# Gating the first two chunks as one group, first fills on VectorE, and weight loads cut into column pieces

## The chip, the cores and the metric

The kernel runs on one core of one Trainium2 chip. The metric is the device time of one execution in microseconds (us), lower is better. Five engines work side by side, each on its own instruction stream in order: TensorE (PE, with its weight loads shown as PEld), VectorE (DVE), ScalarE (ACT), GpSimd (POOL) and SyncE (SP). SP and POOL also issue the DMAs.

## What is computed

The reference has two blocks. The first is a gated linear attention over 4 sequences of 768 steps, 8 heads of 48 channels: a complex gate per step and channel, limited in magnitude, decays a 48x48 state, and each output is the query times the state. The second is a mixer on the 384-wide result.

```python
mag = sqrt(a_re*a_re + a_im*a_im)
scale = minimum(mag, 0.999) / (mag + 1e-06)
a = (a_re + 1j*a_im) * scale
for t in range(768):                       # per batch, head
    S = a[t][:, None] * S + outer(k[t], v[t])
    y[t] = q[t] @ S.real
x = y as (batch, 768, 384)
u = x + ((x.T @ U) @ V).T                  # U: 768x32, V: 32x768
out = u + maximum(u @ w_ch1, 0) @ w_ch2    # 384x1536, 1536x384
```

The four mixer weights arrive as 64-bit doubles and are turned into 32-bit floats on the chip.

## The kernel before

**Chunks.** Each sequence is cut into six chunks of 128 steps, 24 in all. A chunk passes through these steps. *Gates* (`gates`): magnitudes through squares, Ln and Exp on ScalarE with adds on VectorE, sums over blocks on TensorE (`es ps`, `tot`), then angles (Arctan on ScalarE, a running sum on TensorE into `ph`, wrapped into `F`), then sine and cosine into `cs`. *Prep* (`prep`): queries and keys weighed by `es`, multiplied by `cs` into `QKC`, transposed by TensorE (`tr`) and copied to `QK` by ScalarE. *Levels and rest* (`chain`): many small products (`inner`, `corners`, `ks ps`, `dk`, `y`), with VectorE rescaling `QK` in place between them, end in `xo`.

**Gates come in groups.** `GROUPS` says which chunks are gated together: `(0, 1)`, `(1, 2)`, then pairs. For a pair each ScalarE and VectorE step is one 768-wide instruction, for a single chunk a 384-wide one. Each group loads two ScalarE function tables (`switch`), one for magnitudes and one for angles.

**The mixer** (`mixer`) takes two chunks at a time once a whole sequence has its `xo`: `mixed`, `uTp`, then the long products `up` and `down`. Later mixers use schemes with fewer products (`few`). Weights (`single`) are loaded by SP as raw doubles into one of two `raw` buffers in `stage`, 768 KB each for the six pieces of `w1` and the six of `w2`. Six VectorE instructions rebuild the float's high part and a correction, and a DMA from POOL adds the correction to `w` in place.

**The order of everything** is made by a planner that runs when the kernel is built (`Plan`). Every operation is entered with an engine, an assumed duration, an urgency class and what it reads and writes; the table `URGENCY` gives a number for each class and index, and each engine takes the most urgent ready operation. The result is one fixed stream per engine. Where the planner expects TensorE to have nothing to do before the first `mixing` operation has been planned, it puts a filler in the stream, a 128x128 product of the identity with itself named `spare` (`idle`, line 1232). Fillers are real instructions: TensorE executes all of them in order, whether it would have been idle or not.

**The start.** POOL sets up `ident`, fills the constant parts of `QKC`, the three `T`, two `AT` and two `DG` tiles (lines 392 to 407), and only then makes `mid` and `total` from the loaded `prefix` (lines 415 to 434).

Of the kernel before, what the change touches and what calls it, by code (L numbers as in the profile page):

```python
# [12 lines left out]
U32 = mybir.dt.uint32  # L13
# [9 lines left out]
GC = 2  # L23
# [3 lines left out]
    "w1": {0: 577.09, 1: -1319.32, 2: 484.43, 3: -236.69, 4: 471.82, 5: -1058.73, 6: 187.51},  # L27
    "w2": {0: -111.09, 2: 522.21, 4: 896.97, 6: -52.37, 8: 604.14, 10: 640.8, 12: -317.28},
    "gates": {0: -265.04, 1: 268.17, 2: 43.76, 4: -996.63, 6: 89.37, 8: 509.61, 10: -55.71, 12: 809.99, 14: -95.12,
        16: 160.61, 18: -122.91, 20: -425.54, 22: -1729.17},  # L30
    "angles": {0: -126.72, 1: -84.17, 2: -1567.87, 4: -1150.68, 6: -325.13, 8: 105.31, 10: 61.73, 12: 732.88,
        14: -1148.2, 16: 655.25, 18: 538.84, 20: -116.45, 22: 233.15},
    "prep": {0: -1639.87, 1: -367.99, 2: -1022.47, 3: -12.47, 4: -106.92, 5: -436, 6: -74.87, 7: 260.1, 8: -1682.29,
        9: 278.7, 10: 47.08, 11: 569.46, 12: -1452.21, 13: -249.3, 14: -287.97, 15: -363.52, 16: -269.7,
        17: -1664.43, 18: -240.93, 19: 153, 20: -1089.48, 21: -198.95, 22: -127.5, 23: 757.32},
    "levels": {0: 731.75, 1: -318.03, 2: 17.02, 3: -430.68, 4: -436.08, 5: -170.38, 6: 221.56, 7: 124.72, 8: -1567.59,
        9: -1453.16, 10: -1698.36, 11: -60.78, 12: 502.58, 13: 523.21, 14: -1475.59, 15: 515.81, 16: -1265.88,
        17: 487.77, 18: -263.92, 19: 16.81, 20: 723.89, 21: -1759.83, 22: -1111.46, 23: -160.12},
    "rest": {0: 468.93, 1: -1086.12, 2: 24.25, 3: -218.54, 4: -1119.41, 5: -346.92, 6: 0.68, 7: -1700.8, 8: 681.55,
        9: -376.72, 10: -229.72, 11: -305.85, 12: -1069.62, 13: 601.71, 14: -282.72, 15: 204.95, 16: 59.77,  # L40
        17: 552.08, 18: -62.45, 19: 466.03, 20: -1105.96, 21: -351.77, 22: -1688.33, 23: 463.92},
# [147 lines left out]
def kernel(  # L189
# [47 lines left out]
    GROUPS = [(0, 1), (1, 2)] + [(n, n + GC) for n in range(2, NT, GC)]  # L237
    NG = len(GROUPS)

    PAIRED = 6  # L240
# [5 lines left out]
    AT_ONCE = (0, 1, 2, 3)  # L246
    WP = 768

# [64 lines left out]
    def SP(cost, *a, **kw):  # L313
        plan.add("SP", max(cost, 0.65), *a, late=2.0 if cost > 0.65 else 1.4, **kw)
# [77 lines left out]
    nc.gpsimd.memset(QKC, 0.0)  # L392
# [5 lines left out]
    for n in range(3):  # L398
        TS.append(singles.tile([DQ, GC, H * NTOT], FP, name="T%d" % n))
        nc.gpsimd.memset(TS[n], 1.0)  # L400
    for n in range(3):
        VP.append(singles.tile([128, H, D], FP, name="VP%d" % n))
    for n in range(2):
        AT.append(singles.tile([128, H, HC], FP, name="AT%d" % n))
        DG.append(singles.tile([128, H, BLK], FP, name="DG%d" % n))
        nc.gpsimd.memset(AT[n], 0.0)
        nc.gpsimd.memset(DG[n], 0.0)
# [37 lines left out]
    def load_a(g):  # L445
        lo, hi = GROUPS[g]
        for nm, src in (("ar", a_re), ("ai", a_im)):
            for i in range(lo, hi):
                SP(c_dma(DM), ("load", (0, 0.5, 3)[g] if g < 3 else lo + 3), lambda nm=nm, src=src, i=i: nc.sync.dma_start(
                    out=get(nm, g)[:, i - lo], in_=rows(src, i)), writes=[(nm, g, i)])  # L450
# [12 lines left out]
    def single(p, rank, to, o, pieces):  # L463
# [12 lines left out]
        for a, at, end in zip(pieces, ends, ends[1:]):  # L476
            SP(c_dma(2 * (end - at)), rank_l, lambda a=a, at=at, end=end: nc.sync.dma_start(
                out=get("raw", p)[:, at:end].rearrange("p (c m) two -> p c (m two)", c=a.shape[1]), in_=a.bitcast(U32)),
               writes=[("raw", p, at)])
# [51 lines left out]
    def gates(g):  # L531


        lo, hi = GROUPS[g]
        W = (hi - lo) * DM
        R1, R2 = ("gates", lo), ("angles", lo)
        ca, cd = c_act(W), c_dve(W)
        x, y, l, n, z, ar, ai = names = [(nm, g) for nm in ("x", "y", "l", "n", "z", "ar", "ai")]

        def t(b):  # L540
            a = get(*b)
            return (a.rearrange("p c h d -> p (c h d)") if b[0][0] == "a" else a)[:, 0:W]

        def of(b, i):
            return get(*b)[:, (i - lo) * DM:(i - lo + 1) * DM]

        def magnitudes():
            ring(l, "GL", GL)
            ACT(ca, R1, lambda: act(t(x), t(ar), AF.Square), [ar], [x])
            ACT(ca, R1, lambda: act(t(y), t(ai), AF.Square), [ai], [y])  # L550
            DVE(cd, R1, lambda: add(t(x), t(x), t(y)), [y], [x])
            DVE(c_one(W), R1, lambda: nc.vector.tensor_scalar(out=t(x), in0=t(x), scalar1=M2LO, scalar2=M2HI, op0=OP.max,
                                                              op1=OP.min), [], [x])
            ACT(ca, R1, lambda: act(t(n), t(ar), AF.Abs), [ar], [n])
            table(ca, R1, lambda: act(t(l), t(x), AF.Ln), [x], [l])
            table(ca, R1, lambda: act(t(x), t(l), AF.Exp, scale=0.5), [l], [x])
            DVE(cd, R1, lambda: add(t(x), t(x), t(n)), [n], [x])
            table(ca, R1, lambda: act(t(y), t(l), AF.Exp, scale=-0.5, bias=leps), [l], [y])
            table(ca, R1, lambda: act(t(y), t(y), AF.Ln, bias=1.0), [], [y])

            ACT(ca, R1, lambda: act(t(l), t(l), AF.Relu, scale=-0.5, bias=lmax), [], [l])
            DVE(cd, R1, lambda: nc.vector.scalar_tensor_tensor(out=t(l), in0=t(l), scalar=LNMAX, in1=t(y), op0=OP.subtract,
                                                               op1=OP.add), [y], [l])
            table(ca, R1, lambda: act(t(x), t(x), AF.Ln), [], [x])
            table(ca, R1, lambda: act(t(x), t(x), AF.Exp, scale=-1.0), [], [x])
            DVE(cd, R1, lambda: mul(t(x), t(x), t(ai)), [ai], [x])
            ACT(ca, R1, lambda: act(t(n), t(ar), AF.Sign, bias=tiny), [ar], [n])
            for i in range(lo, hi):
                within(i)

        def within(i):
            ps, es = ("es ps", i), ("es", i)
            psum(ps, "T", [128, DM], [128, 512])
            buffer(es, "es", 3, [128, 2, DM])
            PE(0.65, R1, lambda: nc.tensor.matmul(out=get(*ps), lhsT=mid, rhs=of(l, i), start=True, stop=True),  # L575
               [l, ("mid", 0)], [ps, ("sums", g, i)], takes=[es], steps=2)
            for u in range(2):
                table(c_act(DM), R1, lambda u=u: act(get(*es)[:, u], get(*ps), AF.Exp, scale=1.0 - 2 * u), [ps], [es + (u,)])

        def totals():  # L580
# [3 lines left out]
            for i in range(lo, hi):  # L584
                of_blocks(i)
# [6 lines left out]
        def of_blocks(i):  # L592
# [15 lines left out]
        def turns():  # L608

            table(ca, R2, lambda: act(t(x), t(x), AF.Arctan), [], [x])  # L610
            DVE(cd, R2, lambda: nc.vector.scalar_tensor_tensor(out=t(z), in0=t(x), scalar=math.pi / 4, in1=t(n),  # L611
                                                               op0=OP.subtract, op1=OP.mult), [x, n], [z])
            ACT(ca, R2, lambda: act(t(z), t(z), AF.Identity, scale=1.0 / math.pi, bias=fourth), [], [z])
            for i in range(lo, hi):
                angles(i)

        def angles(i):
# [6 lines left out]
            first = i < NCH  # L624
            if where(i)[1] > 0 and not first:
                POOL(1.0, R2, lambda: nc.gpsimd.dma_start(out=of(z, i)[0:1], in_=fo(i - 1)[CH - 1:CH], accum_op=OP.add),
                     [("F", i - 1)], [zi], late=2.6)
# [3 lines left out]
            carry = first and i > 0  # L631
# [9 lines left out]
        def waves():  # L641
            cs = ("cs", g)
            buffer(cs, "cs", 2, [128, GC, H, 2, D])

            def half(u):
                return get(*cs).rearrange("p c h u d -> p (c h) u d")[:, 0:W // D, u]
            fs = [("F", i) for i in range(lo, hi)]
            ft = heads(F.rearrange("p c m -> p (c m)")[:, lo % GC * DM:lo % GC * DM + W])
            ACT(ca, R2, lambda: act(half(0), ft, AF.Abs), fs, [cs + (0,)])
            table(ca, R2, lambda: act(half(1), ft, AF.Sin, scale=2.0 * math.pi), fs, [cs + (1,)])  # L650
            table(ca, R2, lambda: act(half(0), half(0), AF.Sin, scale=-2.0 * math.pi, bias=quarter), [], [cs + (0,)])
# [9 lines left out]
    def prep(i):  # L661
        R1 = "prep", i
        g = group_of(i)
        qk, QK = ("qk", i), ("QK", i)
        buffer(QK, "QK", 3, [DQ, 2, H, CH])
# [4 lines left out]
        for u in range(2):  # L670
# [4 lines left out]
                [qk, ("cs", g)], [qkc])  # L675
# [521 lines left out]
    for g in range(NG):  # L1197
# [8 lines left out]
        if g:  # L1206
            totals()
        else:
            later = [totals]
# [78 lines left out]
```

## Time and profile before

| | before |
|---|---|
| median of 3 runs | 705.47 us (704.29 to 705.83) |
| profiled execution, its own time | 704.41 us |
| span of the profile (first to last instruction) | 702.6 us |
| PE busy | 681.1 us, 97% |
| of it fillers (`spare`) | 61.4 us, 219 products |
| DVE / ACT / POOL busy | 540.1 / 418.1 / 51.8 us |
| mean granted TensorE clock | 0.990 of full |

In the profile every 32-bit matmul shows as two records, so 438 `spare` records are 219 products. Busy time counts overlapped records once. "Issue" is time in which an engine waited for nothing that the profile shows.

### The profile page before, as it was taken

The page shows a single profiled execution, that of the slowest core. Times are in us where ns is not written, and L with a number is a line of the kernel's source. Part 1 is how long each engine was busy: PE and PEld are TensorE (multiplying, and loading weights), DVE is VectorE, ACT ScalarE, POOL GpSimd, SP SyncE. Part 2 cuts the span into 40 slices and gives each one's busy share as a digit, 9 for nine tenths or more (in the row PEclk, how much of TensorE's full clock was granted, in tenths as well). Part 3 has the DMA queues.
Part 4 walks back from the last instruction along what each step waited for, and adds up shares of the span by engine and source line. Part 5 has one row for each costly group of instructions (what it writes and reads, how often), then busy time and mean ns, then how long its engine had stood idle before and what let it go on. Part 6 is the DMA issues. An engine that isn't in the chain of part 4 may idle for free.

```text
span 702.6 us, 27047 instructions
## 1 busy us (share of the span) xinstructions
PE 681.1 (97%) x12148; PEld 601.0 (86%) x12148; DVE 540.1 (77%) x877; ACT 418.1 (60%) x778; POOL 51.8 (7%) x92
## 2 busy tenths in 40 slices
PE   7989998999999999999999999999999999999998
PEld 6877877877688888879888888889999999899997
DVE  5899998888898887759678487879887787455734
ACT  6786987678797687977784953651624415041230
POOL 5110000011000010001000000000000000000000
PEclk9999999799999999999999999999999999999999
DMA  7876855498424343252334032040121000000000
GB/s 185 172 184 149 186 103 141 91 209 176 99 51 90 68 94 76 41 109 53 63 77 93 9 67 59 10 98 26 23 42 35 14 27 17 18 7 24 7 18 22
DMA packets 165267, 53.24 MB, mean 76 GB/s; under 512 B 154080, under 2 KB 160416, under 8 KB 165152
## 3 DMA queue, kind: packets, MB, share of 16 engines
q1 hardware_dynamic: 161072, 42.26, 27.7%
q0 software_dynamic: 4080, 9.27, 5.6%
q8 instruction: 95, 1.56, 0.9%
q14 instruction: 20, 0.16, 0.1%
HBM read 33.59 MB, written 4.72 MB: 55 GB/s over the span
## 4 chain that ended last, share of the span: by engine, by line
PE 79%; ACT 9%; DVE 7%; issue 3%; DMA 1%; SPq 0%; DVEq 0%; ACTq 0%
PE down L1105 21%; PE few L974 12%; PE up L916 12%; PE inner L716 6%; PE tr L682 5%; ACT gate L326 3%; PE dk L802 3%; PE y L841 3%; PE spare L1232 2%; PE ks ps L787 2%; PE down L1062 2%; PE es ps L575 2%; PE ph L632 2%; PE tot L601 2%; PE y L833 2%
## 5 line engine op out<-in xcount | busy, mean ns | idle before, releaser
L329 DVE TENSOR_TENSOR QK<-QK,T 112x1024 f32<-112x1024 f32 x120 | 145.8, 1221 | 6.5 <-PE corners L766 5.3
L916 PE MATMUL up<-uT,w 128*128 128x256 f32 x432 | 98.7, 381 | 0.0
L916 PEld LDWEIGHTS up<-uT,w 128*128 128x128 f32 x432 | 80.7, 190 | 12.0 <-DVE uT L906 0.2
L326 ACT ACTIVATE gate<-gate 128x768 f32<-128x768 f32 (+1 forms) x91 | 71.0, 792 | 6.2 <-DVE gate L611 2.0
L1105 PE MATMUL down<-w,h 128*128 128x192 f32 x396 | 73.2, 330 | 0.0
L982 ACT COPY h<-few 128x512 f32<-128x512 f32 x36 | 20.8, 584 | 85.2 <-PE few L974 85.1
L685 ACT COPY QK<-tr 112x512 f32<-112x512 f32 x96 | 52.0, 588 | 32.6 <-PE tr L682 32.3
L1105 PEld LDWEIGHTS down<-w,h 128*128 128x128 f32 x396 | 63.9, 190 | 2.7 <-issue 1.3
L1232 PE MATMUL spare<-ident 128*128 128x128 f32 x438 | 61.4, 289 | 2.1 <-POOL ident masks.py:199 1.5
L332 DVE TENSOR_TENSOR h<-few,h 128x512 f32<-128x512 f32 x54 | 37.2, 691 | 30.2 <-PE few L974 26.2
L1232 PEld LDWEIGHTS spare<-ident 128*128 128x128 f32 x438 | 55.1, 198 | 5.9 <-issue 1.9
L716 PEld LDWEIGHTS inner<-QK 112*32 112x32 f32 x4608 | 45.9, 110 | 16.4 <-issue 10.7
L716 PE MATMUL inner<-QK 112*32 112x16 f32 (+1 forms) x4608 | 51.2, 190 | 4.9 <-issue 4.5
L682 PE MATMUL tr<-ident,QKC 128*112 128x128 f32 x384 | 51.9, 275 | 1.2 <-ACT QK L685 0.8
L329 DVE TENSOR_TENSOR QKC<-qk,cs 128x768 f32<-128x768 f32 x48 | 45.9, 956 | 9.3 <-PE tr L682 6.6
L332 DVE TENSOR_TENSOR xo<-down,xo 128x192 f32<-128x192 f32 (+1 forms) x79 | 29.8, 388 | 27.0 <-PE down L1105 25.2
L682 PEld LDWEIGHTS tr<-ident,QKC 128*112 128x112 f32 x384 | 42.3, 133 | 6.1 <-ACT QK L685 1.8
L974 PE MATMUL few<-gate,w 128*128 128x128 f32 x336 | 43.1, 277 | 0.0
L1049 POOL DMA_DIRECT2D out_dram<-xo x32 | 17.9, 560 | 338.9 <-DVE xo L332 278.8
L850 ACT COPY xo<-y 64x192 f32<-64x192 f32 x96 | 30.1, 313 | 19.2 <-PE y L841 16.0
L722 DVE COPY_PREDICATED DG<-mask,inner 128x128 f32<-128x128 int32 (+1 forms) x72 | 24.6, 344 | 20.4 <-PE inner L716 20.3
L974 PEld LDWEIGHTS few<-gate,w 128*128 128x128 f32 x336 | 40.0, 192 | 0.3
(131 smaller groups left out, 1272.0 us busy)
## 6 DMA issues: line engine op xcount, KB each, us to landing
stage<-in_moe_w_ch_dram SPq DMA_DIRECT2D x12, 768.0 KB, 6.5
gate<-in_a_re_dram SPq DMA_DIRECT2D x24, 192.0 KB, 3.2
gate<-in_a_im_dram SPq DMA_DIRECT2D x24, 192.0 KB, 4.3
qk<-in_q_dram SPq DMA_DIRECT2D x24, 192.0 KB, 4.0
qk<-in_k_dram SPq DMA_DIRECT2D x24, 192.0 KB, 4.4
VP<-in_v_dram SPq DMA_DIRECT2D x24, 192.0 KB, 3.3
w<-stage POOLq DMA_DIRECT2D x12, 384.0 KB, 5.7
T<-E SPq DMA_DIRECT2D x44, 96.0 KB, 2.5
```

The lines of the kernel that those rows point to most:

```text
L326: return nc.scalar.activation(out=o, in_=i, func=f, **kw)
L329: nc.vector.tensor_tensor(out=o, in0=a, in1=b, op=OP.mult)
L332: nc.vector.tensor_tensor(out=o, in0=a, in1=b, op=OP.add)
L682: nc.tensor.transpose(out=get(*ps)[0:DQ, j], in_=get(*qkc)[:, hh * HH + j].rearrange("p u d -> p (u d)")[:, 0:DQ], identity=ident)
L685: ACT(c_act(HH * CH) - 0.05, R1, lambda u=u, hh=hh, ps=ps: nc.scalar.copy(out=get(*QK)[:, u, hh * HH:(hh + 1) * HH], in_=get(*ps)[0:DQ]), ...
L716: nc.tensor.matmul(out=get(*ps)[js, h], lhsT=k_of(h)[:, js], rhs=part(q_of(h)[:, js], "p"), start=True, stop=True, tile_position=(0, j * BLK))
L722: nc.vector.copy_predicated(out=to, mask=part(mask[:, n], "p").unsqueeze(1).to_broadcast(list(to.shape)), data=a if hf < 8 else a.rearrang ...
L850: ACT(c_act(HH * D), RR, lambda r=r, u=u: nc.scalar.copy(out=get(*xi).rearrange("p (a u d) -> p a u d", u=2, d=D)[r * HC:(r + 1) * HC, :, ...
L916: nc.tensor.matmul(out=get(*ps)[:, e], lhsT=w1[:, f, (ff + e) * 128:(ff + e + 1) * 128], rhs=get(*uT)[:, f], start=(f == 0), stop=(f == KD ...
L974: nc.tensor.matmul(out=get(*ps)[:, q], lhsT=w()[:, q * 128:(q + 1) * 128], rhs=v[0](), start=(n == 0 and q == 0), stop=True, skip_group_ch ...
L1105: nc.tensor.matmul(out=get(*to)[:, part], lhsT=x(j), rhs=y[:, j], start=(first and j == 0), stop=(j == KH - 1), skip_group_check=not first)
L1232: nc.tensor.matmul(out=spare[0], lhsT=ident, rhs=ident, start=True, stop=True)
```

## The change

- `GROUPS` becomes twelve pairs; the first two chunks are now one group with one pair of table loads. Inside that group, `PARTS` keeps the two chunks as separate 384-wide instructions with their own urgencies; all other groups have one part of 768.
- Totals of the first group are no longer put off until after the next group's table load.
- `PAIRED` and `AT_ONCE` move by one, since group numbers moved by one; they mean the same chunks as before.
- The eight first fills go from POOL to VectorE.
- A weight load becomes four DMAs of 192 doubles per row (192 KB each) in place of one of 768 KB.
- The gate loads of both first chunks lead SP's stream.
- `URGENCY` has new numbers throughout, so every engine's stream is ordered anew.

```diff
-    "w1": {0: 577.09, 1: -1319.32, 2: 484.43, 3: -236.69, 4: 471.82, 5: -1058.73, 6: 187.51},
+    "w1": {0: 646.97, 1: 441.39, 2: -1086.15, 3: 866.49, 4: 669.69, 5: 511.71, 6: 120.17},
...
-    GROUPS = [(0, 1), (1, 2)] + [(n, n + GC) for n in range(2, NT, GC)]
+    GROUPS = [(n, n + GC) for n in range(0, NT, GC)]
+    PARTS = [[(n, n + 1) for n in range(GC)]] + [[g] for g in GROUPS[1:]]
-    PAIRED = 6
+    PAIRED = 5
-    AT_ONCE = (0, 1, 2, 3)
+    AT_ONCE = (0, 1, 2)
+    SPLIT = 192
...
-    nc.gpsimd.memset(QKC, 0.0)
+    nc.vector.memset(QKC, 0.0)
...
-        nc.gpsimd.memset(TS[n], 1.0)
+        nc.vector.memset(TS[n], 1.0)
...
-        nc.gpsimd.memset(AT[n], 0.0)
-        nc.gpsimd.memset(DG[n], 0.0)
+        nc.vector.memset(AT[n], 0.0)
+        nc.vector.memset(DG[n], 0.0)
...
-                SP(c_dma(DM), ("load", (0, 0.5, 3)[g] if g < 3 else lo + 3), ...
+                SP(c_dma(DM), ("load", i / 20 if g == 0 else 3 if g == 1 else lo + 3), ...
...
+            m = a.shape[2]
+            if m <= SPLIT:
...
+            for c in range(a.shape[1]):
+                for lo in range(0, m, SPLIT):
+                    hi = min(lo + SPLIT, m)
+                    o_at = at + c * m + lo
+                    SP(c_dma(2 * (hi - lo)), rank_l, lambda ...: nc.sync.dma_start(
+                        out=get("raw", p)[:, o_at:o_at + hi - lo], in_=a[:, c, lo:hi]...),
+                       writes=[("raw", p, o_at)])
...
-        if g:
-            totals()
-        else:
-            later = [totals]
+        totals()
```

Built, the two kernels differ in these instruction counts: 196 fillers for 219; 24 table loads for 26; 8 fills on VectorE and none of these on POOL; 48 weight loads for 12 (beside the two of U and V); 48 stores of totals for 52. Every other kind of instruction has the same count and size, and the streams differ in order.

## The prediction

> **What bounds the kernel now.** I read the page's busy times and slices first, then the windows by stage, then PE's waits and the timeline at the places where PE stood still.
>
> ```profile
> PE 681.1 (97%) x12148; PEld 601.0 (86%) x12148; DVE 540.1 (77%) x877; ACT 418.1 (60%) x778; POOL 51.8 (7%) x92
> ...
> PE   7989998999999999999999999999999999999998
> DVE  5899998888898887759678487879887787455734
> ...
> PEclk9999999799999999999999999999999999999999
> ...
> L1232 PE MATMUL spare<-ident 128*128 128x128 f32 x438 | 61.4, 289 | 2.1 <-POOL ident masks.py:199 1.5
> ```
>
> PE looks full from the start, but 61.4 of its 681.1 us are fillers, and all fillers stand before the first `up`. Full rows of DVE lie in the same stretch, and the clock row has one slice below full.
>
> ```profile
> 0.00:20.00 20.00, 14.99 (x107) 13.37 (x108) 11.05 (x25) 12.41 (x23) 10.65 (x33) 0.91 0.82 190
> 20.00:112.00 92.00, 85.33 (x1896) 72.44 (x1894) 87.61 (x129) 74.91 (x137) 6.29 (x7) 1.00 0.70 155
> ...
> 116.00:119.00 3.00, 0.00 (x1) 0.00 (x0) 1.43 (x2) 2.83 (x4) 0.00 (x0) 1.00 0.49 136
> ...
> 120.40:130.70 10.30, 9.98 (x204) 8.31 (x193) 8.66 (x11) 3.80 (x12) 0.00 (x0) 0.50 0.31 72
> 130.70:152.00 21.30, 21.04 (x456) 17.11 (x455) 18.66 (x30) 15.19 (x31) 2.89 (x3) 1.00 0.66 136
> 152.00:650.00 498.00, 495.56 (x8940) 437.23 (x8939) 381.53 (x619) 293.25 (x551) 30.31 (x46) 1.00 0.27 58
> ```
>
> The columns after the length are PE, PEld, DVE, ACT and POOL busy, granted clock, DMA share, GB/s. From 152 us on PE has 2.4 us of idle in 498: that part is bound by PE's real work, which the change leaves alone. From 20 to 112 DVE is busy 95% of the time. So the time is decided by how early the first mixer can start, and in that front part DVE (then ACT) sets the pace while PE pads with fillers.
>
> ```profile
> PE inner L716 <- issue: 4.5, 3, 3.1
> ...
> PE es ps L575 <- DVE mask L440: 3.6, 1, 3.6
> ...
> 5.83 1.73 DVE L552 TENSOR_SCALAR gate<-gate 128x384 f32<-128x384 f32 x1
> ...
> 11.13 1.53 PE L575 MATMUL es ps<-GL,mid 128*128 128x384 f32 x2 [3.56 <-DVE mask L440]
> ...
> 119.11 0.45 PE L716 MATMUL inner<-QK 112*32 112x32 f32 x30 [3.10 <-issue]
> ...
> 152.24 7.93 PE L916 MATMUL up<-uT,w 128*128 128x256 f32 x36
> ```
>
> PE has two long stops. At 7.6 us it has run out of fillers and waits 3.6 us for the first `GL` (the row names the `mask` instruction that DVE ran right behind it). At 116 us it stops 3.1 us in the middle of a row of `inner` while nothing in the profile holds it ("issue"). Two 768 KB weight loads, issued at 109.3, fill the DMA engines just then (DMA share 0.94 at 112 to 116), and a block of instructions is fetched by DMA inside the stop. The clock then runs at half from 120.4 to 130.7.
>
> **Part 1: the fillers and the first group.** PE executes each filler in order, so the number of them is a cost that can be counted. 219 products took 61.4 us, 0.28 each. The changed stream has 196, all again before the first `up`, with one `ph` less ahead of it: 23 x 0.28 = -6.4 us. The count is only the planner's opinion of PE's idle time, so I check it on the two engines that PE waits for, counting the stream of each up to the first mixer step with this profile's durations. ACT: two table loads less (2 x 1.28) and 4.3 us of gate work and one `F` moved behind that point, -6.9 us. DVE: two weight conversions fewer (2 x 4.15, four instructions of 0.56 and two of 0.96), and about 1.5 us of gate and `F` work moved behind, -9.8 us. All three have the same sign. The order inside changes: chunk 0's `cs` comes after both chunks' magnitudes, ten more ACT instructions of about 0.52 (some in waits), near 25 us for 20.8; chunk 1's `cs`, at 42 us before, near 28; and the gate loads of chunks 2 and 3, issued at 28 to 33 before, come forward with it.
>
> **Part 2: the fills.** POOL loses 4 x 0.95 + 2 x 0.52 + 2 x 0.31 = 5.5 us. `total` ended at 10.2; now POOL is free at 2.3 and waits for `prefix`, which stands behind two more gate loads on SP. I put `mid` at about 8, with `es ps` needing it at 12: covered. DVE gains 5632 elements of MEMSET, which the trace does not show at this size. The nearest rows are DVE's TENSOR_SCALAR, 0.56 us for 768, which gives 4.1 us in all, and POOL's own 5.5. The Trainium skill, "VectorE: DVE Perf Modes", section "Zero memsets can be issued as uint32 (trn2)", says a memset takes one cycle per element whatever the type. With 0.96 GHz (its page "Trainium Kernel Development and Optimization") that is an estimated 5.9. DVE was idle from 1.0 to 5.2, so by the rows the first add is late by 0 to 1.3 us, by the rule by 1.7. I take the rule, since the fast TENSOR_SCALAR row has no fill near it. Against it stands the 1.73 us that one 384-wide TENSOR_SCALAR took while POOL filled; its twin at 19.85 took 0.36. With POOL quiet 1.4 comes back, so the first Ln is about level. Then the first `es ps`: x ready at 7.8, eight ACT instructions (about 3.9, two of them the other chunk's) and one DVE, 12.3. PE reaches it after 30 fillers at 1.5 + 6.1 + 10 x 0.28 = 10.4. It waits about 2 us in place of 3.6: -1.5. Ends: 0 and -3.6.
>
> **Part 3: the pieces.** Bytes are the same. 36 more DMAs on SP at 0.45 us median are 16 us of SP time, 18 of them before 100 us. A rule speaks against this: the Trainium skill, "DMA: Bandwidth & Descriptors", section "Anatomy of one DMA - SWDGE (gpsimd) path", has a fixed cost of about 2.0 us per DMA; in series it would be 72 us. The row: four `AT<-DG` copies are issued in 2.6 us though each takes 1.9 to land, so fixed costs overlap on this queue. I take SP's 0.45 each, hidden, since SP spends its time waiting (97 us for `DG` alone). Without that cover, behind a piece wait gate loads, q, k, v and the `T` and `AT` copies; each load would be late by 3 x 0.45 = 1.4 us. The conversion still waits for all four pieces, so a weight by itself is not earlier. What pieces allow is that other loads go between: in the new stream the first pieces that follow the six of `w1` stand after `VP`, `V` and an `AT` copy.
>
> **Part 4: the stop at 116 us.** It costs 3.1 us, and 10.3 us at half clock, 5.1 of PE's time: 8.2. The Trainium skill, "TensorE: Matmul & The Clock Gate", section "Part 1: The HAM clock gate (the "warmup" mystery)", would have full clock back after one busy window of about 3.4 us: 1.7 lost, 4.8 in all. The window row says 10.3, so 8.2. Is it still there? In the old stream both weight loads meet a run of `inner`, `tr` and `dk`, where instructions are smallest and are used up fastest. In the new stream the pair comes after chunk 3's `VP` buffer is free, that is after its `y`, when the densest run is past. So I take the stop as gone or short (other issue waits before `inner` average 0.36 us). Ends: 0 and -8.2.
>
> **Sum.** By PE: -6.4 - 1.5 = -7.9, with part 4 up to -16.1. DVE caps this. It has 9.8 less to do, starts 1.7 to 2.3 later, about -7.5; of its idle time after the stop (1.6 + 0.6 + 1.6 up to 130.7) at most 3.8 goes too: -11.3. I take -10. Profiled execution 704.4 - 10 = 694.4. The median of the runs stands 1.1 above it: 695.5 us.
>
> **Rivals.** *A, as above*: 695.5, own range 690 to 699, chance 0.56. *B, the stop stays or comes elsewhere*: weights still arrive in pairs of 1.5 MB, and pieces of one load go out back to back, so the instruction fetch may meet them as before. Then only parts 1 and 2 count, -6 to -8: 698.5. For it: ten blocks of the new stream are still dense; against: about seventeen were. Chance 0.24. *C, the front does not get shorter*: chunk 0's `inner` starts near 32 us for 27.7, SP's extra issues delay the next gate loads, and the fillers are simply replaced by idle time: -3 to +1, 703.5, chance 0.12. *D, slower: `down` waits for `w2`.* The two conversions taken out of the front now stand behind it: five between the first mixer add and the last `w2`, not three. With the rest of DVE's stream there that is about 33 us, for 22.7 before. POOL's add needs 5.7 more to land. By my count PE wants the last `w2` about 40 us after its first `up` and gets it at about 38; before, the spare time was about 4. If a pair of loads or DVE is late by 5 us, `down` waits 3.5 and the clock falls as at 116 us: 8.6 lost. That alone takes back A's gain. It decides the sign from two such waits, 17 us: 712. Chance 0.08. That the change does nothing of what it says is excluded for groups and fills; for the pieces it is the case that no load passes between them, which is in B.
>
> **How the numbers follow.** A difference of about 0.2% (1.4 us) is what a measurement of this kernel can tell from none. Faster: A, B, two thirds of C and a little of D, 0.90; same: 0.04 from C and D; slower: 0.06, mostly D. The range reaches from 688 (A with most of part 4 on PE's account) to 703 (most of C), leaving out 2 in 10.
>
> **What would show it.** Right: `spare` near 55 us; the first `up` at about 142 us for 152.2; no stop over 1 us near 110 us and no half-clock slice after it; `es ps` waiting about 2 us at 10; MEMSET rows of about 1.07 us on DVE; chunk 1's sine and cosine near 28 us. Wrong: a stop with "issue" and half clock (B), `up` at 150 or later (C), PE waiting for `w` at `down` (D), or PE's idle time after `up` above 10 us.

## The result and the profile after

| | before | changed |
|---|---|---|
| median of the runs | 705.65 us (704.29 to 708.86, 4 runs) | 697.47 us (696.94 to 700.27, 4 runs) |
| ratio, 95% interval | | 0.9886 [0.9843, 0.9928] |
| profiled execution, span | 704.41, 702.6 us | 700.27, 698.5 us |
| PE busy, of it fillers | 681.1, 61.4 us | 674.6, 55.7 us |
| first `mixed`, first `up` | 144.91, 152.24 us | 132.38, 139.50 us |
| from first `up` to the end | 550.4 us | 559.0 us |

The change is worth 8.2 us by the medians. The profiled execution of the changed kernel is its longest of the four, so where the part behind the first `up` matters I also use three relatives of it from the experiments below, which keep PE's stream: there that part takes 556.5 to 557.4 us.

The page of the changed kernel, busy times, slices and the filler group:

```profile
PE 674.6 (97%) x12102; PEld 593.0 (85%) x12102; DVE 543.2 (78%) x885; ACT 413.4 (59%) x776; POOL 47.3 (7%) x84
...
PE   8998898999999999999998999999999999999998
...
PEclk9999999999999999999999999999999999999999
...
L1263 PE MATMUL spare<-ident 128*128 128x128 f32 x392 | 55.7, 289 | 1.5 <-POOL ident masks.py:199 1.5
```

The slice below full clock is gone, and fillers take 5.7 us less. The windows by stage (columns as in the prediction):

```profile
0.00:20.00 20.00, 17.04 (x140) 15.97 (x141) 15.19 (x34) 15.01 (x31) 5.76 (x24) 1.00 0.73 176
20.00:112.00 92.00, 82.32 (x2056) 69.83 (x2056) 86.69 (x127) 74.42 (x133) 5.35 (x6) 1.00 0.68 146
112.00:144.00 32.00, 30.93 (x647) 25.18 (x640) 28.33 (x41) 19.78 (x42) 3.69 (x4) 1.00 0.67 160
...
152.00:650.00 498.00, 491.21 (x8922) 431.19 (x8921) 381.24 (x620) 290.81 (x550) 30.05 (x46) 1.00 0.26 57
```

The clock is full throughout the front, but from 152 to 650 us PE is idle for 6.8 us, against 2.4 before. The timeline (start, length, then in brackets the idle time ahead and what ended it) at the places that the prediction named:

```profile
1.20 0.91 DVE L394 MEMSET QKC<- 128x1024 f32 x1 [0.18 <-issue]
12.10 0.88 PE L594 MATMUL es ps<-GL,mid 128*128 128x384 f32 x2 [1.42 <-DVE GL L581]
41.40 1.53 PE L594 MATMUL es ps<-GL,mid 128*128 128x384 f32 x4 [0.35 <-DVE GL L581]
139.50 10.63 PE L950 MATMUL up<-uT,w 128*128 128x256 f32 x48
184.08 0.91 PE L594 MATMUL es ps<-GL,mid 128*128 128x384 f32 x2 [1.09 <-ACT QK L719]
373.36 0.31 PE L750 MATMUL inner<-QK 112*32 112x16 f32 x14 [2.06 <-issue]
```

The first `es ps` waits 1.4 us; the long stop near 116 us is absent; the sums for chunks 2 and 3 (`es ps` with four matmuls) stand at 41.40. In the kernel before, the timeline has them here:

```profile
51.17 1.56 PE L575 MATMUL es ps<-GL,mid 128*128 128x384 f32 x4 [1.13 <-DVE GL L562]
```

So 9.8 of the 12.7 us by which `up` comes earlier are already there at 41 us.

### The profile page after: what moved, and what is told of

Same layout as the page of the kernel before. It is cut to its first block, busy times and chain, and to the rows that moved or that the text cites. A ratio compares the mean times of both kernels' runs of the same rounds, so it can differ in the third digit from the quotient of the medians.

```text
span 698.5 us, 26976 instructions
## 1 busy us (share of the span) xinstructions
PE 674.6 (97%) x12102; PEld 593.0 (85%) x12102; DVE 543.2 (78%) x885; ACT 413.4 (59%) x776; POOL 47.3 (7%) x84
## 3 DMA queue, kind: packets, MB, share of 16 engines
q8 instruction: 95, 1.56, 0.9%
## 4 chain that ended last, share of the span: by engine, by line
PE 76%; DVE 10%; ACT 9%; issue 3%; SPq 1%; DMA 1%; DVEq 0%; ACTq 0%
PE down L1139 21%; PE up L950 12%; PE few L1008 12%; PE inner L750 5%; PE tr L716 5%; ACT gate L328 4%; PE dk L836 3%; PE y L875 2%; PE ks ps L821 2%; PE es ps L594 2%; DVE QK L331 2%; PE ph L661 2%; PE tot L623 2%; PE y L867 1%; PE spare L1263 1%
## 5 line engine op out<-in xcount | busy, mean ns | idle before, releaser
L950 PE MATMUL up<-uT,w 128*128 128x256 f32 x432 | 100.8, 387 | 0.0
L1263 PE MATMUL spare<-ident 128*128 128x128 f32 x392 | 55.7, 289 | 1.5 <-POOL ident masks.py:199 1.5
L716 PE MATMUL tr<-ident,QKC 128*112 128x128 f32 x384 | 53.3, 276 | 2.6 <-DVE QKC L331 1.7
L331 DVE TENSOR_TENSOR QKC<-qk,cs 128x768 f32<-128x768 f32 x48 | 45.7, 952 | 12.7 <-PE tr L716 11.2
L1263 PEld LDWEIGHTS spare<-ident 128*128 128x128 f32 x392 | 49.9, 199 | 4.7 <-POOL ident masks.py:199 1.5
L328 ACT ACTIVATE h<-up 128x512 f32<-128x512 f32 x36 | 21.4, 595 | 31.4 <-PE up L950 31.4
```

Of the source, the lines that this page charges most:

```text
L328: return nc.scalar.activation(out=o, in_=i, func=f, **kw)
L331: nc.vector.tensor_tensor(out=o, in0=a, in1=b, op=OP.mult)
L716: nc.tensor.transpose(out=get(*ps)[0:DQ, j], in_=get(*qkc)[:, hh * HH + j].rearrange("p u d -> p (u d)")[:, 0:DQ], identity=ident)
L950: nc.tensor.matmul(out=get(*ps)[:, e], lhsT=w1[:, f, (ff + e) * 128:(ff + e + 1) * 128], rhs=get(*uT)[:, f], start=(f == 0), stop=(f == KD ...
L1263: nc.tensor.matmul(out=spare[0], lhsT=ident, rhs=ident, start=True, stop=True)
```

## The experiments

Time and ratio are those of each kernel against the kernel before on the same chip; the interval is 95%. "Front" is the time to the first `up`, "back" the span less that; both are of the one profiled execution of each kernel. The edits are shown abridged.

| kernel | median us | ratio | front | back |
|---|---|---|---|---|
| before | 704.5 to 705.7 | 1 | 152.2 | 550.4 |
| before, pair of loads moved | 705.08 | 1.0014 [0.9998, 1.0030] | 152.2 | 550.9 |
| before, fills on VectorE | 705.14 | 1.0009 [0.9991, 1.0026] | 151.2 | 550.8 |
| before, loads in pieces | 701.69 | 0.9954 [0.9939, 0.9969] | 146.8 | 550.0 |
| before, 23 fillers less | 711.78 | 1.0108 [1.0078, 1.0138] | 150.8 | 559.2 |
| before, 64 fillers less | 705.11 | 0.9998 [0.9983, 1.0013] | 151.9 | 551.5 |
| changed | 697.47 | 0.9886 [0.9843, 0.9928] | 139.5 | 559.0 |
| changed, fills on POOL | 698.71 | 0.9903 [0.9879, 0.9928] | 139.9 | 557.0 |
| changed, loads whole | 700.17 | 0.9933 [0.9909, 0.9956] | 140.5 | 557.8 |
| changed, later conversions cut | 698.43 | 0.9897 [0.9871, 0.9923] | 140.4 | 556.5 |
| changed, front conversions cut | 697.63 | 0.9895 [0.9878, 0.9912] | 138.1 | 557.4 |
| changed, 28 fillers less | 705.32 | 1.0000 [0.9983, 1.0017] | 142.1 | 560.6 |
| changed, 64 fillers less | 701.38 | 0.9946 [0.9925, 0.9967] | 142.1 | 556.4 |
| changed, old urgencies | 727.17 | 1.0310 [1.0282, 1.0338] | 172.2 | 553.8 |

### The stop at 116 us: move the loads, or cut them

First, the kernel before with only the two 768 KB loads that were issued at 109 us moved on SP.

```diff
     # SP's order alone, at the emission
-    load p8, load p9, AT<-DG x4
+    AT<-DG x4, load p8, load p9
```

> The kernel before, with the two 768 KB weight loads that SP issued at 109.3 us moved behind the next four AT<-DG copies, to about 125 us; nothing else moves. If these loads delay the fetch of instructions and so make the stop at 116 us, the stop shrinks to under 1 us, the half-clock slice goes, and the time falls by 5 to 8 us to 698 to 700. If PE had only been stopped ahead of a wait for VectorE, the stop goes but waits appear: -1 to -3. If the dense run of small products makes the stop without the loads, it stays: within 1 us of before.

The time is level. Its timeline and windows around the new place of the loads:

```profile
122.41 1.11 SPq L477 DMA_DIRECT2D stage<-in_moe_w_ch_dram  x2
...
134.82 0.24 PE L833 MATMUL y<-VP,AT 64*64 64x48 f32 x1 [3.33 <-issue]
```

```profile
122.40:131.50 9.10, 7.95 (x247) 6.69 (x248) 8.32 (x13) 5.20 (x10) 0.00 (x0) 1.00 0.96 245
131.50:134.80 3.30, 0.00 (x0) 0.00 (x0) 1.49 (x2) 1.12 (x5) 0.00 (x0) 0.79 0.75 133
```

The loads left 13.1 us later, and the stop came 15.7 us later, as long as before (3.33 for 3.10 us), at another instruction (`y`, not `inner`), with the DMA engines 96% busy ahead of it. So the stop belongs to the pair of loads, not to the place in the program. The level time alone would have fitted the third forecast, that the loads have nothing to do with it; the timeline speaks against that. Next, the loads stay where they were but go out in four pieces each.

```diff
-    nc.sync.dma_start(out=raw[:, at:end], in_=a)          # 768 KB
+    for c, lo in pieces of 192 doubles:                   # 4 x 192 KB
+        nc.sync.dma_start(out=raw[:, o_at:o_at + 192], in_=a[:, c, lo:lo + 192])
```

> The kernel before with each 768 KB weight load issued as four DMAs of 192 doubles per row, back to back at the same place of SP's stream. If only SP's issue time counts (0.45 us each, hidden): no change, within 1 us, and the stop at 116 us stays at about 3 us with its half-clock slice. If smaller pieces let the instruction fetch through, the stop shrinks below 1 us: -5 to -8. If SP's time or a fixed cost of each DMA counts, gate loads land later by 1.4 us each: +1 to +4.

The timeline of this kernel between 115 and 124 us:

```profile
115.95 0.45 PE L724 MATMUL inner<-QK 112*32 112x32 f32 x30 [0.67 <-issue]
...
119.53 0.32 PE L841 MATMUL y<-VP,AT 64*64 64x48 f32 x6 [0.81 <-issue]
...
123.00 0.25 PE L724 MATMUL inner<-QK 112*32 112x16 f32 x6 [1.07 <-issue]
```

Three short stops stand in the place of the long one, and the clock stays full. The first `up` is 5.4 us earlier, the span 5.8 us shorter; by the medians of all runs it is 2.8 us, which is the better measure, since the profiled execution of this kernel is the fastest of its 21 runs. That is about half of what was forecast for shorter stops. In the changed kernel the same cut is undone, each load whole in the slot of its first piece:

```diff
-    SP(..., dma_start(out=raw[:, o_at:o_at + 192], in_=a[:, c, lo:hi]))
+    SP(..., dma_start(out=raw[:, at:end], in_=a) if first piece else None)
```

> The changed kernel with each weight load whole again, issued where its first piece was; all other orders are held. If the pieces bring nothing by themselves: within 1 us of 697.5. If they are what keeps instruction fetches short: stops of 2 to 3 us with a half-clock slice return before the first up, 702 to 706.

It is 2.7 us slower than the changed kernel by the medians, but the two intervals overlap, and neither forecast was met. There is no "issue" stop above 1.6 us (the longest, 1.55, at `dk`): here the whole loads are issued 6 us apart, not as a pair. So the new order alone also removes the long stop.

### The fills

```diff
-    nc.gpsimd.memset(QKC, 0.0)          # the kernel before; and TS, AT, DG
+    nc.vector.memset(QKC, 0.0)
```

> The kernel before with the eight first fills on VectorE in place of GpSimd; all other instructions and orders are the same. By the prediction's second step the first add is later by 1.7 us and the slow TENSOR_SCALAR (1.73 us) falls to about 0.4: level, -0.5 to +0.5 us in the end. Rival: the front is carried by the first Ln alone, and the whole shift of the first es ps, up to 1.4 us either way, is seen at the end.

The reverse, in the changed kernel (VectorE's fills back to POOL):

> The changed kernel with the eight first fills back on GpSimd; all other instructions and orders as in the changed kernel. If the fills gave nothing by themselves: 697 to 698, within 0.5 us of the changed kernel. If they carry part of the gain (GpSimd free early for mid and total, no slow TENSOR_SCALAR): 698.5 to 700, with the first es ps about 1.5 us later.

Both are within 1.3 us of their partner, inside the intervals. The slow TENSOR_SCALAR did fall, from 1.73 to 0.38 us in the kernel before with the fills moved, but the move of the fills is worth nothing that these runs can tell.

### Do the fillers cost their time?

In the first of these, 23 of the old kernel's 219 fillers are left out, spread evenly, with all else held.

```diff
     for n in plan.order():
+        if n < 0 and this is one of 23 evenly spaced: continue
         (plan.ops[n][4] if n >= 0 else idle)()
```

> The kernel before with 23 of its 219 fillers left out at even distances; every other instruction and all orders are the same. If a filler is a cost by itself (0.28 us each on TensorE, as the prediction's first step counted), the time falls by 6.4 us to about 699, and the first up comes at about 146. If VectorE and ScalarE set the pace of the front part and the number of fillers only mirrors that, the gaps turn into waits: 0 to -2 us, and PE's idle time before the first up grows by about 5 us.

It got slower by 7.3 us, which neither forecast had. The front is 1.5 us shorter, but the back grew by 8.8. The timeline of its back has three stops that the kernel before lacks:

```profile
215.37 0.34 PE L716 MATMUL inner<-QK 112*32 112x32 f32 x17 [1.60 <-issue]
...
469.79 0.25 PE L716 MATMUL inner<-QK 112*32 112x32 f32 x3 [1.43 <-issue]
...
523.54 0.33 PE L716 MATMUL inner<-QK 112*32 112x32 f32 x16 [1.50 <-issue]
```

The first two are followed by 3.4 us at half clock. To see what fixes the place of such a stop, count PE's records up to its end with a window from 0 (the first bracket is PE's matmul records). In order: before, to the end of the stop at 116; 23 fillers less, to the ends of two stops; the moved pair, to the end of its stop; and the changed kernel with 28 fillers less, from below, to the end of one.

```profile
0.00:119.11 119.11, 104.06 (x2129) 89.12 (x2129) 103.94 (x159) 94.11 (x168) 16.94 (x40) 0.99 0.72 165
```

```profile
0.00:121.33 121.33, 105.08 (x2129) 89.80 (x2129) 104.63 (x161) 93.91 (x168) 16.91 (x40) 0.96 0.71 162
0.00:124.71 124.71, 107.70 (x2255) 91.99 (x2255) 107.29 (x165) 94.94 (x172) 16.91 (x40) 0.96 0.69 158
```

```profile
0.00:134.82 134.82, 117.59 (x2636) 100.95 (x2636) 119.32 (x180) 102.53 (x190) 16.91 (x40) 0.99 0.69 155
```

```profile
0.00:110.26 110.26, 93.17 (x2129) 79.17 (x2129) 100.68 (x159) 89.37 (x163) 11.00 (x30) 1.00 0.70 153
```

2129 three times, in three different programs; 2255 is 126 further, and 2636 four times 126.75 further. The "issue" stops sit at fixed counts of PE's own instructions, about 127 matmuls and their 127 weight loads apart, whatever the program does there. The page of the kernel before shows what happens at such a count:

```profile
q8 instruction: 95, 1.56, 0.9%
```

95 fetches bring 1.56 MB of instructions, 16 KB each (12,148 matmuls and as many weight loads are 94.9 times 256), and in the traces one starts 2.3 to 3.0 us ahead of the end of each of these stops and takes 0.9 to 1.6 us. The Trainium skill, "Runtime: NRT & Kernel Launch", section "Instruction fetch mechanics", says that instructions come in blocks of 16 KiB, 256 instructions, while the block before is executed, at a cost that is mostly hidden. The block fits the spacing. "Mostly hidden" holds where a block lasts long: in none of the 14 traces do two of these fetches start less than 3.2 us apart, and behind blocks that PE used up in 1.3 to 3.8 us it stands for 0.5 to 3.3 us, though not at every such border.

This also shows what the pair of loads does. In the kernel before, the fetch that ends the long stop takes 0.94 us, like others, but it starts 4.2 us after PE has passed the border ahead of it, at 112.5 us; at the other borders from 60 us to the mixer it is 0.7 to 2.5 us. With the loads in pieces it starts 1.6 us after that border.

So a filler left out moves every later block border by two matmul records. That can be tested with two counts: 28 products are 56 records, which puts the borders of the changed kernel at nearly the worst places, and 64 products are 128 records, one block, which puts them back.

```diff
+        if n < 0 and this is one of 28 (64) evenly spaced, none of the first 54: continue
```

> The changed kernel with 28 of its 196 fillers left out, evenly from the 55th on; the other orders are held. From the changed kernel's trace I took the time that PE spends on each stretch of 127 matmul records that ends at such a place, and call a stretch under 2.6 us short of its difference. In the order as it is they add up to 4.1 us; moved by 28 products (56 records) to 11.1, nearly the worst of all positions, and all of it behind the first `up`. Theory (place): +5 to +9 over the changed kernel, about 704.5, and the part from the first `up` to the end 562 to 566 for 556 to 559. Rival 1 (each filler costs 0.28 us): 7.8 less, about 690. Rival 2 (fewer fillers slow it by themselves, 0.32 us each): +9, about 706.

> The changed kernel with 64 of its 196 fillers left out, evenly from the 55th on; the other orders are held. By the same sum over stretches this position has 4.3 us for 4.1 in the order as it is. Theory (place): more fillers are gone than in the run with 28 fewer, and still it is within -4 to +2 of the changed kernel, about 697, with 556 to 559 from the first `up` to the end. Rival 1 (each filler costs 0.28 us): 17.9 less, about 680. Rival 2 (fewer fillers slow it by themselves): +20, about 717.

> The kernel before with 64 of its 219 fillers left out, evenly from the 45th on; the other orders are held. In the traces so far the short "issue" stops of PE lie at fixed places of its own instruction stream, 127 matmul records apart (2001, 2128, 2255 and 2509 records in the kernel with 23 fillers less; 2129 for the 3.1 us stop before), wherever those fall in the program; 64 products are 128 records, so behind the fillers the places fall on the same instructions as before. Theory (place, not number, of the fillers): the part from the first `up` to the end, 550.4 us before and 559.2 with 23 fewer, is 550 to 552 again; the front is paced by VectorE and comes out 0 to 4 us shorter; time 700 to 705. Rival 1 (each filler costs its 0.28 us): 64 x 0.28 = 17.9 less, about 687. Rival 2 (fewer fillers slow the kernel by themselves, 7.3 us for 23 as measured): about +20, 725.

With 28 fewer the changed kernel takes 705.32 us, its whole gain is gone (its ratio's interval lies clear of the changed kernel's); with 64 fewer 701.38. The first time alone would fit place and count alike (704.5 and 706 forecast); the second tells them apart. The old kernel with 64 fewer takes 705.11: level, though PE has 64 products less to execute. Two stops in the back of the kernel with 28 fewer:

```profile
367.39 0.25 PE L750 MATMUL inner<-QK 112*32 112x32 f32 x3 [2.28 <-issue]
...
387.34 0.18 PE L750 MATMUL inner<-QK 112*32 112x16 f32 x1 [1.41 <-issue]
```

Its back is 560.6 us, that with 64 fewer 556.4, and the old kernel's with 64 fewer 551.5 for 550.4: number does not decide, place does, at least in the back. In the front it is otherwise. The changed kernel with 64 fewer lost 3.9 us where -4 to +2 was forecast, and both runs with fewer fillers reach the first `up` at 142.1 us, not earlier but later than the changed kernel and its relatives (138.1 to 140.5); so of the 7.9 us that 28 fewer cost, about 4 in the back (560.6 for 556.4) go to the place. With 64 fewer PE is idle more often, as these windows show (PE was busy 36.33 and 45.99 us there in the changed kernel), and the clock falls to half for 13.7 us in three stretches.

```profile
20.00:60.00 40.00, 30.77 (x621) 23.41 (x621) 33.36 (x47) 29.17 (x51) 2.78 (x3) 0.91 0.82 182
60.00:112.00 52.00, 42.40 (x1259) 34.61 (x1250) 51.43 (x77) 45.15 (x83) 2.56 (x3) 0.97 0.55 113
```

A filler thus costs the front next to nothing and helps to keep PE's clock up; that a count was good or bad for the time lay in the block borders.

### Does VectorE pace the front?

The changed kernel with three weights' conversions in the front cut to one of six instructions, 9.6 us of VectorE work left out.

```diff
+        heavy = p not in (3, 4, 5)
-        DVE(one, rank, lambda: nc.vector.tensor_scalar(out=x(), in0=hi(), ...
+        DVE(one, rank, (lambda: nc.vector.tensor_scalar(out=x(), in0=hi(), ...) if heavy else nothing
```

> The changed kernel, with the weight conversions of the pieces 3, 4 and 5 of w1 (done on VectorE between some 25 and 90 us) cut to one of their six VectorE instructions each: 15 instructions, 4 x 0.56 + 0.96 = 3.2 us each time, 9.6 us of VectorE left out ahead of the first mixer; w1 is wrong with it. All orders, fillers and DMAs are held, so PE's instruction blocks stand where they were. It measures the step by which the changed front is thought to be shorter, VectorE's work there (119.9 us busy of 132.4 up to the first `mixed`, for 125.8 of 144.9 before). Theory (VectorE paces the front): the first `up` comes 5 to 9 us earlier than the 139.5 to 140.5 of the changed kernel, at 131 to 135, the part behind it stays at 556 to 559, time 689 to 693. Rival (ACT, the loads or PE itself with its 196 fillers pace it): 138.5 to 140.5, and 696 to 698.

The rival was right in the main (138.1 us for its 138.5 to 140.5). Windows of this kernel, and its first `up`; the same window of the changed kernel had 50.20 us of DVE:

```profile
60.00:112.00 52.00, 46.96 (x1364) 40.26 (x1367) 46.17 (x67) 41.67 (x81) 2.56 (x3) 1.00 0.59 118
```

```profile
138.09 10.63 PE L954 MATMUL up<-uT,w 128*128 128x256 f32 x48
```

Of 9.6 us (7.4 by VectorE's busy time up to the first `up`), 1.4 reach the first `up`. In the chain of waits up to the first `up`, pieces on DVE fall from 43.9 to 35.3 us while pieces on PE rise from 43.8 to 60.4, fillers among them (9.5 to 15.3). The chain of the kernel before could have warned of it: of its 152.2 us up to the first `up`, 26.3 are pieces on DVE, 46.6 on ACT and 55.9 on PE. An engine that is busy 95% of a stretch need not be what the stretch waits for: what one engine gives up here, the next takes.

### The work behind the first `up`, and the numbers of the order

Five later weights' conversions cut in the same way (16 us of VectorE left out, behind the first mixer):

```diff
+        heavy = p < 8
```

> The changed kernel, where the last five pieces of w2 keep only one of the six VectorE instructions that rebuild them (25 instructions, 16 us of VectorE left out; these weights are therefore not rebuilt). If the conversions moved behind the first mixer are what makes PE wait again after the first up (0.63 us and 0.46 us for QKC at 172 and 179, 1.09 us for QK at 184 in the changed kernel's profile), those waits go and the time falls by 2 to 3 us to about 695. If they are set by something else (ScalarE, PSUM buffers), no change within 0.7 us.

The back is 556.5 us, no shorter than its relatives', so the conversions that the change put behind the first `up` are not what takes time there. Last, the changed kernel with the old `URGENCY` numbers, planned anew (280 fillers):

```diff
-    "w1": {0: 646.97, 1: 441.39, ...},        # and all other rows
+    "w1": {0: 577.09, 1: -1319.32, ...},
```

> The changed kernel with the old URGENCY numbers; the planner orders anew and puts in 280 fillers. If the gain belongs to the grouping, fills and pieces by themselves: at or below the kernel before, 695 to 705. If the gain belongs to structure and table together, and fillers tell the length of the front part: 84 x 0.28 = 23 us above the changed kernel, about 721.

It is 29.7 us slower than the changed kernel, where 23 was forecast from its 84 additional fillers; its first `up` comes at 172.2. Since leaving fillers out saved nothing in either kernel, they are hardly the reason, but that was not tested here. One group for the first two chunks, fills and pieces together bring no shorter time without the new order. The reverse, the new numbers in the old structure, was not run.

## Why the prediction was right, and where it was not

**The time.** 695.5 was predicted, 697.47 measured, inside the range and inside rival A's own. That is in part luck. The 10 us were set by a cap from VectorE's work (-7.5) and by the end of the long stop (-3.8); the runs bear out neither. The front gained 12.7 us, for a reason that stood in part 1 only as a change of order, and the part behind it, taken as unchanged, lost 6 to 7.

**Part 1, the fillers: the step "the number of them is a cost that can be counted" failed.** The change's own count was right (55.7 us, 5.7 less for 6.4), but leaving 64 out saved no time in either kernel, and leaving 23 out cost 7.3 us. The check on the other two engines failed as well where it set a cap from VectorE's work: 9.6 us less of it brought 1.4. What did happen is narrower. The milestones, from the timelines:

| start, us | before | before, pieces | changed, old urgencies | changed |
|---|---|---|---|---|
| first gate step of chunks 2 and 3 on ACT | 36.83 | 36.22 | 32.86 | 31.65 |
| their first Ln (into `GL`) | 43.54 | 42.92 | 37.74 | 35.67 |
| their `es ps` | 51.17 | 50.55 | 48.55 | 41.40 |
| first copy to `xo` | 77.78 | 77.19 | 98.64 | 65.38 |
| last copies to `xo` ahead of the mixer | 143.47 | 138.26 | 159.89 | 130.44 |
| first `up` | 152.24 | 146.82 | 172.22 | 139.50 |

Nearly ten microseconds are won before 41 us, 12.4 by the first copy to `xo`, and no more than 0.6 after that. Chunk 1's sine and cosine were done at 29.4 us (42 before; predicted 28), and the gate loads of chunks 2 and 3 were issued at 22.0 to 27.3, not 28.2 to 33.1. The chain of waits of the kernel before has that load as a link:

```profile
32.36 4.25 DMA gate<-in_a_im_dram
```

In the changed kernel's chain this link is gone. SP had waited 3.0 us with these loads for chunk 1's gate work on ACT, which the kernel before does behind a table load of its own. The kernel with the old urgencies shows how the ten divide. It has the joint group and the loads at 24.1 to 27.8, and it starts the Ln of chunks 2 and 3 5.8 us earlier than the kernel before (7.9 in the changed kernel). From there to `es ps` the kernel before needs 7.6 us, the old numbers 10.8 and the new ones 5.7. With the pieces alone it starts 0.6 us earlier, so up to that Ln most of the gain comes with the joint group; the new order decides that it is kept.

**The first `es ps`.** A wait of about 2 us from 10.4 on was predicted; 1.42 us up to 12.10 came. But counting the shorter wait as 1.5 us won was wrong: `es ps` began 0.97 us later than before (12.10 for 11.13), with 30 fillers ahead of it for 20, so the wait was filled, not shortened. **Part 2, the fills.** The rule's price held: a 1024-wide fill took 0.91 us and the next began 1.07 after it, and the fills ended at 7.0. The end of it, nothing gained or lost, held in both kernels.

**Part 3, the pieces.** Costing them at nothing was the mis-sized term: in the old kernel they brought 0.46% [0.31, 0.61], about 3 us; in the changed kernel 2.7 us by the medians, not clear of the intervals. They gain by what part 4 is about, a shorter stop, not by letting other loads pass. The fixed cost per DMA did not add up over 36 more DMAs; the section that gives it is on the path from POOL, and these are SP's.

**Part 4, the stop.** It was there for the reason named, a fetch of instructions that meets the pair of loads; the moved pair shows it. Its worth was given as 0 to 8.2: with it gone the old kernel's span fell by 5.8 us and its median by 2.8. In the changed kernel it is gone, and six stops of 0.6 to 1.0 us stand in the front instead. The stretch in which the long stop stood, from the first copy to `xo` to the last ones ahead of the mixer, takes 65.7 us before, 61.1 with pieces alone and 65.1 in the changed kernel: of what the end of the stop was worth, almost nothing is seen there.

**What was not foreseen: part of the gain is given back.** The step that failed is that the part from 152 us on is one "which the change leaves alone". The first `up` came 12.7 us earlier, 2.5 more than predicted, but from there to the end the changed kernel takes 6 to 7 us longer in its relatives' profiles (556.5 to 557.4 for 550.4), and 8.6 in its own, which has the 2.06 us stop at 373 and 3.4 us of half clock. PE's idle time from 155 to 650 us rose from 2.4 to 6.0 (with fills on POOL); the timeline shows 2.2 of it at three waits between 172 and 184 us, where `tr` waits for `QKC` and `es ps` for ScalarE, and one `ph` (0.8 us of PE) has moved there. The last line of the prediction named idle time behind `up` as a sign of error, with 10 us as its bound; some 2 us of the return are not accounted for.

**The rivals.** *B* had the right mechanism, but the stop near 116 us did not stay. B's sign, a stop with "issue" and half clock, did come once, at 373 us of the changed kernel's own profile; its three relatives have at most 0.8 us there. *C* was wrong: the front is shorter. *D* did not occur: no `down` waited for `w` by more than 0.9 us in any profile of the changed order, and cutting the conversions brought nothing. The gain could have been lost in another way: with 28 fillers fewer it would have been zero.

## What to carry to other kernels

A count of filler instructions, or of one engine's busy time, is a forecast only after one run has shown that taking some away shortens the stage; follow the milestones instead, and see where the gain is made. A stop of TensorE that nothing explains, in the midst of tiny matmuls, is worth a count of the instructions ahead of it: if such stops are a fixed number apart, instructions arrive too late, and a large load just ahead makes it worse. Compare two orders of such code at more than one offset, since any edit ahead moves the borders and may change the time by 1% for no reason of its own.

## What the runs showed of the hardware that was not expected

- Two fetches of PE's instructions never started less than 3.2 us apart in these 14 traces. Blocks that are used up in 1.3 to 3.8 us can leave PE standing, 0.5 to 2.3 us by themselves and 2.9 to 3.3 us behind two 768 KB loads. A bad offset cost 8.8 us in the back of the kernel before and about 4 us in that of the changed one.
- Stops of 1.43 to 1.62 us were followed by 3.4 us at half clock, but one of 1.50 us was not (523 us in the kernel with 23 fillers less), nor one of 2.28 us (367 us, with 28 fillers less). The 3.10 us stop was followed by 10.2 us, the 3.33 us one by 6.8, and one of 1.09 us (110 us, with 28 fillers less) by 10.2. So the length of the stop alone does not decide. The Trainium skill, "TensorE: Matmul & The Clock Gate", section "Part 1: The HAM clock gate (the "warmup" mystery)", asks for at least one busy window of about 3.4 us before the clock is full again; the rows agree in steps of 3.4 us, one, two or three of them.
- In the kernel before, the same bytes in loads of 192 KB (packets of 1.5 KB for 3 or 6 KB) left room for the fetch that two loads of 768 KB delayed. It is not a rule: with the old urgencies a long stop stands behind pieces, and its fetch started 3.2 us after the border.

```profile
129.62 0.37 PE L716 MATMUL tr<-ident,QKC 128*112 128x128 f32 x1 [2.59 <-issue]
```

Whether it is the size of the packets that decides was not tested.
